# A product in the second bank of a PSUM pair, other banks for the last products, and two stores on GpSimd's queue

## Chip, cores and metric

The kernel runs on one core of a Trainium2 chip. The metric is the device time of one execution in microseconds (us), the median of several runs. A core has TensorE (PE in the profile, with PEld for its weight loads), VectorE (DVE), ScalarE (ACT), GpSimd (POOL) and SyncE (SP). Each works through its own list of instructions in order; an instruction waits for counts that the other engines and the DMA queues raise. SP, ScalarE and GpSimd issue DMAs on queues of their own.

## The reference

Retention over 8 batches of 576 positions and 8 heads of 64, then a feed-forward layer on the 4608 x 512 result:

```python
scores = scale * np.matmul(q, k.transpose(0, 1, 3, 2))
Dmat = np.where(rel >= 0, gamma[:, None, None] ** rel[None, :, :], 0.0)
x = np.matmul(scores * Dmat[None, :, :, :], v)      # then (B * S, H * D) = (4608, 512)
...
h = x @ w_in                                        # 4608 x 2048
s = np.sin(alpha * h)
g = h + s * s / (alpha + 1e-09)
return (g @ w_out).astype(np.float32)               # 4608 x 512
```

## The kernel before

The 4608 rows are taken in 9 blocks of 512 (block 8 holds the last 64 positions of all batches). Each block goes through 16 units, one for each 128 of the 2048 columns of h. A unit is: `project`, four matmuls of 128x512 into one PSUM bank (L562); `sine` on ScalarE (L570), which reads that bank; `square` on ScalarE or VectorE (L579, L581); and `product` on VectorE (L586), which reads the square and the bank again and writes g, transposed, to the tile gT.

The second matmul of the layer, g times w_out, is done for blocks 3 to 8 with seven products of half-size matrices instead of eight. The 512x512 result of a block is cut into four quarters, and product i is a group of 16 matmuls of 128x256 that takes a factor on the left made from gT and one on the right made from w_out (L671, `FACTORS` at L654). Left factors S1 to S4 are sums of quarters of gT, made on VectorE by `row_sum` (L652). `after_product` (L700) joins the products: after product 1, ScalarE copies it to the tile low (L703); after 6, VectorE writes mid = product 6 + low (L705); after 7, low is raised (L707); after 2, 3, 4 and 5, a result quarter goes to a store tile osb (ScalarE copy L718, or VectorE add L720) and from there to the output by two DMAs (L684 for the last block, else L688).

PSUM has eight banks. The tags op, h0, h1 and h2 are one bank each; m0 and m1 are pairs, tiles of two banks. The tag names a place: a new tile of a tag waits until the readers of the old one are done. Attention uses the pairs whole. `bank` (L549) gives a unit the first bank of a pair when its tag is m0 or m1; the second bank then lies idle.

Iteration n of the loop over blocks 3 to 8 does the units of block n and, from n = 4 on, the seven products of block n - 1 between them. In iterations 4 to 7 units 0 and 1 take m0 and m1 (`aside`, L1387), and the other units take h0, h1, h2 in turn. After the start of every second unit stands one product (`slots`, L1389): product 1 stands on TensorE behind the projection of unit 1, product 2 behind that of unit 3, product 6 behind that of unit 5. Product 1 takes op. Product 2 is summed onto it in the same bank, once ScalarE has copied product 1; the sum is then copied out by ScalarE. Product 6 takes op next, and 7 is summed onto it; then 5 with 3, and 4, use op in the same way.

Up to units 13 to 15 of an iteration the next block's attention runs too; its results leave PSUM by ScalarE copies (L120), so ScalarE comes late to the sines of the last units and of units 0 and 1 that follow.

Behind the loop (L1398 on) come the seven products of block 8, with the last row sums between them, in the order 2, 4, 1, 6, 7, 5, 3; product 3 is done and stored in two halves. The stores there go half on SP's and half on ScalarE's queue (`both`). In iteration 8, whose units end in the order 8, 9, 10, 11, unit 8 has m0, unit 9 h2, unit 10 h0 and unit 11 m1; the turn of the h banks goes on with h1, h2, h0.

The order of instructions on every engine is the order of the calls in the program; no scheduler changes it.

Of the kernel before, what the change touches and what calls it, by code (L numbers as in the profile page):

```python
# [10 lines left out]
F32 = mybir.dt.float32  # L11
# [25 lines left out]
def kernel(  # L37
# [18 lines left out]
    nc = tc.nc  # L56
# [4 lines left out]
    P = 128  # L61
# [24 lines left out]
    psum = ctx.enter_context(tc.tile_pool(name="p", bufs=1, space=bass.MemoryType.PSUM))  # L86
# [459 lines left out]
    ops = {}  # L546
    PART = {None: slice(0, 512), 0: slice(0, 256), 1: slice(256, 512)}

    def bank(tag):  # L549
        if tag[0] == "m":  # L550
            return psum.tile([P, 2, 512], F32, tag=tag, bufs=1, name="hps")[:, 0]
        return psum.tile([P, 512], F32, tag=tag, bufs=1, name="hps")

    def project(n, fc, tag, part=None):

        if n not in gT:
            gT[n] = work.tile([P, FC, 512], F16, tag="gT", bufs=2, name="gT")
        if (n, fc) not in hps_of:
            hps_of[n, fc] = [bank(tag), None]
        cols = PART[part]  # L560
        for a in range(KT):
            matmul(  # L562
                hps_of[n, fc][0][:, cols], w_in16[fc // 4][:, a, fc % 4 :: 4], xs[n][:, a, cols],
                start=(a == 0 and part != 1), stop=(a == KT - 1), skip_group_check=True,
            )
# [44 lines left out]
    def quarter(n, t, h, p):  # L610
        return gT[n][:, 8 * p + 4 * h : 8 * p + 4 * h + 4, 256 * t : 256 * t + 256]

    def w_quarter(h, e, p):
        return w_out16[:, 8 * p + 4 * h : 8 * p + 4 * h + 4, 256 * e : 256 * e + 256]
# [8 lines left out]
    def piece(name, p):  # L623
        tag = PIECES[name, p]
        if (name, p) not in pieces:
            if tag in ("raw3", "raw5", "xT1"):
                both = work.tile([P, 2, 4, 256], F16, tag=tag, bufs=1, name=name)
                for x in range(2):
                    pieces[name, x] = both[:, x]
            else:  # L630
                pieces[name, p] = work.tile([P, 4, 256], F16, tag=tag, bufs=1, name=f"{name}_{p}")
        return pieces[name, p]
# [11 lines left out]
    def row_sum(n, name, p, eng):  # L644
        a11, a12, a21, a22 = (quarter(n, t, h, p) for t in range(2) for h in range(2))
        out_, x, y, op = {
            "S1": lambda: (piece("S1", p), a11, piece("S2", p), ADD),
            "S2": lambda: (piece("S2", p), a22, a21, SUB),
            "S3": lambda: (a21, a11, a21, SUB),
            "S4": lambda: (piece("S4", p), a12, piece("S2", p), SUB),  # L650
        }[name]()
        return eng.tensor_tensor(out_, x, y, op)  # L652
# [6 lines left out]
    def part_product(n, i, tag, js=(0, 1), first=None):  # L659
        left, right = FACTORS[i]  # L660
        if tag is not None:
            parts[n, i] = bank(tag)
        else:
            parts[n, i] = parts[n, first]
        acc = parts[n, i]
        for j in js:
            for p in range(2):
                lhs = piece(left, p) if isinstance(left, str) else quarter(n, *left, p)
                rhs = piece(right, p) if isinstance(right, str) else w_quarter(*right, p)
                for x in range(4):  # L670
                    matmul(  # L671
                        acc[:, 256 * j : 256 * j + 256], lhs[:, x, 128 * j : 128 * j + 128], rhs[:, x],
                        start=(tag is not None and j == js[0] and p == 0 and x == 0),
                        stop=(p == 1 and x == 3), skip_group_check=True,
                    )

    def store(n, t, e, osb, js=(0, 1), issue=(nc.sync, nc.sync)):
        cols = slice(256 * e, 256 * e + 256)
        for r in range(2):
            if n == 8:  # L680
                b0 = 4 * t + 2 * js[0]
                dst = out.rearrange("(b s) d -> b s d", s=S)[b0 : b0 + 2 * len(js), 512:576, cols]
                dst = dst.rearrange("(j r) s d -> r s j d", r=2)
                issue[r].dma_start(dst[r], osb[halves(r), js[0] : js[-1] + 1])  # L684
            else:
                r0 = 576 * n + 256 * t + 128 * js[0]
                dst = out[r0 : r0 + 128 * len(js), cols].rearrange("(j i r) d -> r i j d", r=2, i=64)
                issue[r].dma_start(dst[r], osb[halves(r), js[0] : js[-1] + 1])  # L688
# [6 lines left out]
    def kept_tile(name):  # L695
        tag = {"low": "qT1", "mid": "u2"}[name]
        kept[name] = work.tile([P, 512], F32, tag=tag, bufs=1, name=name)
        return kept[name]

    def after_product(n, i, js=(0, 1), issue=(nc.sync, nc.sync), apart=False, more=False):  # L700
        acc = parts[n, i]
        if i == 1:
            nc.scalar.copy(kept_tile("low"), acc)  # L703
        elif i == 6:
            nc.vector.tensor_tensor(kept_tile("mid"), acc, kept["low"], ADD)  # L705
        elif i == 7:
            nc.vector.tensor_tensor(kept["low"], acc, kept["mid" if apart else "low"], ADD)  # L707
        else:
            t, e = {2: (0, 0), 3: (0, 1), 4: (1, 0), 5: (1, 1)}[i]
            cols = slice(256 * js[0], 256 * js[-1] + 256)  # L710
            if (n, i) not in kept:
                kept[n, i] = work.tile([P, 2, 256], F32, tag="osb", bufs=4, name="osb")
            osb = kept[n, i].rearrange("p j d -> p (j d)")
            source = kept["mid" if i == 3 else "low"]
            if more:
                nc.vector.tensor_tensor(kept["mid"], acc, kept["mid"], ADD)
            if i == 2 and not apart:
                nc.scalar.copy(osb[:, cols], acc[:, cols])  # L718
            else:
                nc.vector.tensor_tensor(osb[:, cols], acc[:, cols], source[:, cols], ADD)  # L720
            store(n, t, e, kept[n, i], js, issue)
# [60 lines left out]
    with tc.manual_schedule():  # L782
# [5 lines left out]
        first = work.tile([P, 1], F32, tag="first", bufs=1, name="first")  # L788
# [477 lines left out]
        h, m = cycle(("h0", "h1", "h2")), cycle(("m0", "m1"))  # L1266
        ON_A = (4, 5, 6, 8, 9, 10)
        for n in range(3, NBLK):
# [81 lines left out]
            def unit_start(i, u, tag):  # L1350
                project(n, u, tag)
                sine(n, u)
                for f in todo.get(i, []):
                    f()

            def unit_end(i, u, eng):
                if eng is not None:
                    square(n, u, eng)
                product(n, u)
                for f in after.get(i, []):  # L1360
                    f()
# [28 lines left out]
            for i in range(8):  # L1390
                for u in (2 * i, 2 * i + 1):
                    unit_start(u, units[u], aside.get(u) or next(h))
                    if u % 2 and slots[i] is not None:
                        k_ = slots[i]
                        part_product(n - 1, k_, None if k_ in (2, 7, 3) else "op", first={2: 1, 7: 6, 3: 5}.get(k_))
                        after_product(n - 1, k_)
                    unit_end(u, units[u], None if A and u == 13 else V if u in ON_V else A_)
        n = NBLK - 1  # L1398
        both = (nc.sync, nc.scalar)
        part_product(n, 2, "h0")  # L1400
        part_product(n, 4, "h1")
        row_sum(n, "S3", 1, V)
        row_sum(n, "S2", 1, V)
        part_product(n, 1, "op")
        after_product(n, 1)
        part_product(n, 6, "h2")
        row_sum(n, "S1", 1, V)
        after_product(n, 2, apart=True, issue=both)
        row_sum(n, "S4", 1, V)
        after_product(n, 6)  # L1410
        part_product(n, 7, "m0")
        after_product(n, 7, apart=True)
        part_product(n, 5, "h0")
        after_product(n, 4, issue=both)
        after_product(n, 5, more=True, issue=both)
        for j, tag in enumerate(("m1", "op")):
            part_product(n, 3, tag, (j,))
            after_product(n, 3, (j,), both)

# [29 lines left out]
```

## Time and profile before

| what | value |
|---|---|
| median of 3 runs | 300.42 us (300.3 to 303.47) |
| the profiled execution | 300.26 us |
| its span in the profile | 298.5 us |
| granted TensorE clock | 1.0 of full speed |
| DMA packets | 123431, 50.09 MB |

The span runs from the first to the last instruction of the program; the rest of the execution's time lies outside it. Times in the profile are microseconds from the span's start. A row of the timeline has start, length, engine, line, operation, tiles and shapes, how many instructions are merged in it, and in brackets how long the engine stood idle before it and what released it. Matmuls overlap: sixteen of 128x256 are shown with a length of 1.91 us but follow each other at a distance of 1.75 us for the group. SPq and ACTq rows are DMA issues; the length is that of the issue, not of the transfer. In the rows of waits stand the sum, the number and the longest.

### The profile page before, as it was taken

What the parts mean: (1) busy time and instruction counts of PE and PEld (TensorE: products, weight loads), DVE (VectorE), ACT (ScalarE), POOL (GpSimd) and SP (SyncE); (2) the same over time, 40 slices, a digit from 0 to 9 for tenths busy, and PEclk for the clock granted to TensorE, in tenths of its full rate; (3) what the DMA queues carried; (4) which work ended last, traced back from release to release, by engine and by line L of the source; (5) the groups of instructions that cost most, each with busy time, mean ns of one, the idle gap of its engine ahead of it and who ended that gap; (6) DMA issues with size and microseconds to landing.
All of it is one profiled execution on the core that took longest, in us unless ns stands there. A gap on an engine that the chain in (4) does not pass through costs nothing.

```text
span 298.5 us, 8497 instructions
## 1 busy us (share of the span) xinstructions
PE 285.1 (96%) x3480; PEld 184.0 (62%) x3480; DVE 226.6 (76%) x334; ACT 205.1 (69%) x343; POOL 136.3 (46%) x151
## 2 busy tenths in 40 slices
PE   6889999999998999999999999999999999999894
PEld 4666545555454645455777667767666776676583
DVE  2597878788259789687976787669778886977864
ACT  1579935997694877787768876877687657855500
POOL 5684688664788676550596059604940000000000
PEclk9999999999999999999999999999999999999999
DMA  7999999998796678998989887997763103111213
GB/s 210 347 234 209 252 292 316 254 265 234 174 249 164 146 165 178 264 168 178 131 207 183 180 172 186 174 153 178 170 137 91 40 12 78 35 37 35 70 37 107
DMA packets 123431, 50.09 MB, mean 168 GB/s; under 512 B 80384, under 2 KB 121344, under 8 KB 123392
## 3 DMA queue, kind: packets, MB, share of 16 engines
q1 hardware_dynamic: 119440, 44.78, 64.6%
q0 software_dynamic: 2688, 4.19, 7.7%
q10 hardware_dynamic: 1264, 0.58, 0.8%
q8 instruction: 27, 0.44, 0.6%
q14 instruction: 12, 0.10, 0.1%
HBM read 36.75 MB, written 9.44 MB: 155 GB/s over the span
## 4 chain that ended last, share of the span: by engine, by line
PE 77%; ACT 10%; DMA 5%; DVE 4%; issue 2%; SPq 0%; DVEq 0%; ACTq 0%
PE hps L562 35%; PE hps L671 23%; PE ops L605 10%; DMA raw<-in_v_dram 5%; ACT s L570 3%; PE o L427 2%; PE sc L385 2%; ACT xT L120 2%; ACT ss L579 2%; PE kv L321 2%; ACT v L120 1%; PE o L449 1%; DVE osb L720 1%; ACT kvs L120 1%; DVE ss L581 1%
## 5 line engine op out<-in xcount | busy, mean ns | idle before, releaser
L586 DVE SCALAR_TENSOR_TENSOR gT<-ss,inva,hps 128x512 f16<-128x512 f16 x144 | 105.7, 744 | 39.7 <-ACT ss L579 36.1
L570 ACT ACTIVATE s<-hps,alpha_t 128x512 f16<-128x512 f32 x144 | 97.0, 681 | 45.5 <-PE hps L562 45.1
L562 PE MATMUL hps<-xT,w_in 128*128 128x512 f16 (+1 forms) x532 | 121.1, 372 | 0.9 <-DVE ret L397 0.7
L562 PEld LDWEIGHTS <-w_in 128*128 128x128 f16 x596 | 66.6, 114 | 50.7 <-issue 1.4
L579 ACT ACTIVATE ss<-s 128x512 f16<-128x512 f16 x107 | 67.2, 630 | 2.8
L605 PE MATMUL ops<-w_out,gT 128*128 128x512 f16 x192 | 46.8, 380 | 0.0
L671 PEld LDWEIGHTS <-gT 128*128 128x128 f16 x384 | 37.5, 98 | 11.8 <-issue 3.9
L207 POOL TENSOR_TENSOR k<-raw,cn 128x1024 f16<-128x1024 f32 (+1 forms) x17 | 29.8, 1756 | 9.6 <-DMA raw<-in_k_dram 6.7
L671 PEld LDWEIGHTS <-S 128*128 128x128 f16 x288 | 27.7, 98 | 5.3
L605 PEld LDWEIGHTS <-gT 128*128 128x128 f16 x192 | 17.9, 98 | 20.4
L359 POOL TENSOR_TENSOR s<-kvs,cn 128x256 f16<-128x256 f32 x17 | 10.4, 614 | 40.4 <-DVE S L652 36.9
L207 POOL TENSOR_TENSOR q<-raw,cn 128x1024 f16<-128x1024 f32 x13 | 24.6, 1905 | 6.2 <-DMA raw<-in_q_dram 5.3
L671 PE MATMUL hps<-w_out,gT 128*128 128x256 f16 x192 | 22.9, 272 | 2.8 <-DVE gT L586 1.4
L671 PE MATMUL hps<-T,gT 128*128 128x256 f16 x192 | 22.9, 273 | 0.0
L671 PE MATMUL hps<-w_out,S 128*128 128x256 f16 x192 | 22.8, 273 | 0.0
L397 DVE TENSOR_TENSOR ret<-sc,mask 128x1024 f16<-128x1024 f32 x16 | 19.2, 1219 | 1.7 <-PE sc L385 1.7
L367 POOL TENSOR_TENSOR kvs<-s,kvs 128x256 f32<-128x256 f32 x21 | 16.7, 796 | 3.6 <-DVE kvs L122 1.1
L581 DVE TENSOR_TENSOR ss<-s 128x512 f16<-128x512 f16 x29 | 14.7, 509 | 3.1 <-ACT s L570 3.1
L366 POOL TENSOR_TENSOR s<-kvs,cn 128x256 f32<-128x256 f32 x21 | 13.1, 623 | 6.4 <-ACT kvs L120 6.2
L652 DVE TENSOR_TENSOR S<-gT,S 128x1024 f16<-128x1024 f16 x24 | 15.5, 684 | 0.0
L397 DVE TENSOR_TENSOR ret<-sc,mask_halved 128x768 f16<-128x768 f32 x16 | 15.2, 950 | 0.0
L562 PE MATMUL hps<-xS,w_in 128*128 128x512 f16 x64 | 15.1, 379 | 0.0
(82 smaller groups left out, 266.1 us busy)
## 6 DMA issues: line engine op xcount, KB each, us to landing
out_dram<-osb SPq DMA_DIRECT2D x67, 128.0 KB, 2.5
raw<-in_q_dram SPq DMA_DIRECT2D x16, 512.0 KB, 5.3
raw<-in_k_dram SPq DMA_DIRECT2D x8, 512.0 KB, 6.1
raw<-in_v_dram SPq DMA_DIRECT2D x8, 512.0 KB, 6.3
raw<-in_v_dram SPq DMA_DIRECT2D x32, 128.0 KB, 3.4
raw<-in_k_dram SPq DMA_DIRECT2D x32, 128.0 KB, 3.2
w_in<-in_moe_w_in_dram POOLq DMA_DIRECT2D x4, 512.0 KB, 11.7
w_out<-in_moe_w_out_dram POOLq DMA_DIRECT2D x4, 512.0 KB, 13.0
```

What stands on the lines that cost most here:

```text
L207: eng.tensor_tensor(dst[:, a0:a1].rearrange("p a r t d -> p t (a r) d"), t_.rearrange("p (t a) x -> p t a x", t=2)[:, :, a0:a1].rearrange( ...
L366: nc.gpsimd.tensor_tensor(s32, self.kvs[:, c - 1], g1.unsqueeze(2).to_broadcast([P, 4, D]), MULT)
L367: nc.gpsimd.tensor_tensor(self.kvs[:, c], s32, self.kvs[:, c], ADD)
L397: nc.vector.tensor_tensor(ret.rearrange("p t (z x) -> p (t z) x", z=2)[:, :, 0:n], sc.rearrange("p t (z x) -> p (t z) x", z=2)[:, :, 0:n], ...
L562: matmul(hps_of[n, fc][0][:, cols], w_in16[fc // 4][:, a, fc % 4 :: 4], xs[n][:, a, cols], start=(a == 0 and part != 1), stop=(a == KT - 1 ...
L570: nc.scalar.activation(s_t, hps, mybir.ActivationFunctionType.Sin, bias=0.0, scale=alpha_t[:, fc : fc + 1],)
L579: nc.scalar.activation(ss_t, s_t, mybir.ActivationFunctionType.Square)
L581: eng.tensor_tensor(ss_t, s_t, s_t, MULT)
L586: nc.vector.scalar_tensor_tensor(gT[n][:, fc, :], ss_t, inva[:, fc : fc + 1], hps, MULT, ADD)
L605: matmul(ops[n, c, cols.start][:, cols], gT[n][:, fk, c * P : (c + 1) * P], w_out16[:, fk, cols], start=(fk == 0), stop=(fk == FC - 1), sk ...
L652: return eng.tensor_tensor(out_, x, y, op)
L671: matmul(acc[:, 256 * j : 256 * j + 256], lhs[:, x, 128 * j : 128 * j + 128], rhs[:, x], start=(tag is not None and j == js[0] and p == 0 ...
```

## The change

Three edits:

- In iterations 4 to 7, product 1 of the block before goes to the second bank of the pair m1 whose first bank unit 1 holds. Product 2 is then a group of its own in op, and its quarter is made by a VectorE add of product 2 and low in place of the ScalarE copy.
- Behind the loop, products 2, 4, 6, 7, 5 and the first half of 3 take m0, three turns of the h banks, m1 and m0, in place of h0, h1, h2, m0, h0 and m1.
- Product 5's two stores behind the loop are both issued on GpSimd's queue.

```diff
+    pair = {}
+
     def bank(tag):
+        if tag == "m1 second":
+            return pair["m1"][:, 1]
         if tag[0] == "m":
-            return psum.tile([P, 2, 512], F32, tag=tag, bufs=1, name="hps")[:, 0]
+            pair[tag] = psum.tile([P, 2, 512], F32, tag=tag, bufs=1, name="hps")
+            return pair[tag][:, 0]
         return psum.tile([P, 512], F32, tag=tag, bufs=1, name="hps")
...
                     if u % 2 and slots[i] is not None:
                         k_ = slots[i]
-                        part_product(n - 1, k_, None if k_ in (2, 7, 3) else "op", first={2: 1, 7: 6, 3: 5}.get(k_))
-                        after_product(n - 1, k_)
+                        alone = n < 8 and k_ < 3
+                        tag = "m1 second" if alone and k_ == 1 else None if k_ in (2, 7, 3) and not alone else "op"
+                        part_product(n - 1, k_, tag, first={2: 1, 7: 6, 3: 5}.get(k_))
+                        after_product(n - 1, k_, apart=alone and k_ == 2)
...
         both = (nc.sync, nc.scalar)
-        part_product(n, 2, "h0")
-        part_product(n, 4, "h1")
+        part_product(n, 2, "m0")
+        part_product(n, 4, next(h))
...
-        part_product(n, 6, "h2")
+        part_product(n, 6, next(h))
...
-        part_product(n, 7, "m0")
+        part_product(n, 7, next(h))
         after_product(n, 7, apart=True)
-        part_product(n, 5, "h0")
+        part_product(n, 5, "m1")
         after_product(n, 4, issue=both)
-        after_product(n, 5, more=True, issue=both)
-        for j, tag in enumerate(("m1", "op")):
+        after_product(n, 5, more=True, issue=(nc.gpsimd, nc.gpsimd))
+        for j, tag in enumerate(("m0", "op")):
             part_product(n, 3, tag, (j,))
             after_product(n, 3, (j,), both)
```

Lines of the changed kernel stand 5 below those of the kernel before up to the loop: `sine` is L575 there, the product groups L676, low L708, the adds to osb L725, the last stores L689.

## The prediction

> **What bounds the kernel now.** I read the page first, then the stages, then TensorE's waits, then single stretches of the timeline. The page's header, the busy line, the chain, and two stages (start:end, length, PE, PEld, DVE, ACT, POOL busy, granted clock, DMA share, GB/s):
>
> ```profile
> span 298.5 us, 8497 instructions
> PE 285.1 (96%) x3480; PEld 184.0 (62%) x3480; DVE 226.6 (76%) x334; ACT 205.1 (69%) x343; POOL 136.3 (46%) x151
> PE 77%; ACT 10%; DMA 5%; DVE 4%; issue 2%; SPq 0%; DVEq 0%; ACTq 0%
> 137.00:268.00 131.00, 129.59 (x1576) 90.77 (x1575) 104.10 (x154) 98.82 (x161) 45.73 (x51) 1.00 0.64 131
> 268.00:298.50 30.50, 24.66 (x194) 19.11 (x191) 20.35 (x33) 8.80 (x14) 0.00 (x0) 1.00 0.23 61
> ```
>
> From 137 to 268 us, where most of the change lies, TensorE stands still for 131.00 - 129.59 = 1.41 us. So there any new TensorE wait is added to the time, and any wait removed comes off it, while a fraction of a microsecond on VectorE or ScalarE hides as long as TensorE need not wait for it. TensorE's waits from 150 us on are only these:
>
> ```profile
> PE hps L671 <- DVE gT L586: 1.4, 1, 1.4
> PE hps L671 <- DVE osb L720: 1.4, 3, 0.6
> ```
>
> Both are aimed at by the change: the three before product 1 (0.58, 0.57, 0.24) and the one at the end (1.43).
>
> **Part 1, product 1 in the second bank of unit 1's pair.** It happens in four iterations, n = 4 to 7. Before, product 1 writes "op" and waits there for VectorE's read of product 4. After, that wait goes. But the list of waits of the two built programs has, at product 1 of iteration 5, the same matmul with another wait:
>
> ```
> before: 4226 L671 Matmult hps<-w_out_74,gT 128x256 [waits DVE_49]
> after:  4226 L676 Matmult hps<-w_out_74,gT 128x256 [waits Activation_49]
> ```
>
> The ScalarE count asked for is the one that the sine of unit 1 reaches. The pair is one tile, and a write into its second half is ordered behind the read of its first half that stands before it in the program. The same holds in iterations 4, 6 and 7. So product 1 now starts when the sine of unit 1 ends. Timeline of TensorE's product 1, and of the sine that covers it, iteration by iteration (start, length, idle before and releaser):
>
> ```profile
> 138.31 1.91 PE L671 MATMUL hps<-w_out,gT 128*128 128x256 f16 x16
> 139.05 0.67 ACT L570 ACTIVATE s<-hps,alpha_t 128x512 f16<-128x512 f32 x1
> ...
> 167.58 0.68 DVE L720 TENSOR_TENSOR osb<-hps,low 128x512 f32<-128x512 f32 x1
> 168.32 1.91 PE L671 MATMUL hps<-w_out,gT 128*128 128x256 f16 x16 [0.58 <-DVE osb L720]
> 168.66 0.67 ACT L570 ACTIVATE s<-hps,alpha_t 128x512 f16<-128x512 f32 x1
> ...
> 198.32 1.91 PE L671 MATMUL hps<-w_out,gT 128*128 128x256 f16 x16 [0.57 <-DVE osb L720]
> 197.42 1.25 ACT L570 ACTIVATE s<-hps,alpha_t 128x512 f16<-128x512 f32 x2
> ...
> 227.34 1.91 PE L671 MATMUL hps<-w_out,gT 128*128 128x256 f16 x16 [0.24 <-DVE osb L720]
> 227.53 0.67 ACT L570 ACTIVATE s<-hps,alpha_t 128x512 f16<-128x512 f32 x1
> ```
>
> The sine of unit 1 ends at 139.72, 169.33, 198.67 and 228.20. The hand-over from the VectorE add (ends 168.26) to TensorE (168.32) took 0.06; I use 0.05 for one from ScalarE. New starts less old ones: 1.46, 1.06, 0.40 and 0.91, together 3.83 us later. The sine itself does not move: in ScalarE's order nothing ahead of it changes, and its own input, unit 1's projection, ends before the wait. The end of this projection is product 1's start less its wait (167.74, for example), so TensorE's new idle times are 1.46, 1.64, 0.97 and 1.15. Bounds: 3.4, if ScalarE, relieved of a copy below, comes to each of these places 0.1 earlier; 4.2, if the hand-over costs 0.1 more. I take 3.83.
>
> Behind the waiting matmul stand units 2 and 3 on TensorE; behind them ScalarE and VectorE, which have work of their own in that time. The product of unit 1 on VectorE (L586) gets a new wait too, for the end of product 1, since it reads the same pair. It costs nothing: it already follows the square of unit 1, which stands behind the copy of product 1 in ScalarE's order. The next user of m1, the scores of unit 5, waits for that copy, some 5 us old by then.
>
> **Part 2, product 2 on its own in "op".** Four ScalarE copies to the store tile become four VectorE adds. Rows of a grouping by line for 137 to 232 us, and of the tile low:
>
> ```profile
> L718 ACT COPY osb<-hps 128x512 f32<-128x512 f32 x3 | 1.8, 589 | 1.6 <-PE hps L671 1.6
> L720 DVE TENSOR_TENSOR osb<-hps,low x13: 681/691/694, 155.3 to 293.0; 128x512 f32<-128x512 f32 x13
> ```
>
> ScalarE loses 4 x 0.59, VectorE gains 4 x 0.69. What can wait for it is product 6, which takes "op" next. The tightest place is iteration 7, which has no scores between:
>
> ```profile
> 232.70 1.29 DVE L652 TENSOR_TENSOR S<-gT,S 128x1024 f16<-128x1024 f16 x2
> 234.28 0.93 PE L671 MATMUL hps<-T,S 128*128 128x256 f16 x7
> ```
>
> The new add follows these row sums, which end at 233.99; VectorE is put back by about 0.5 there (by the new wait of unit 1's product), so the add ends near 234.5 + 0.7 = 235.2. Product 6 would start at 234.28 + 0.91 = 235.19. A tie: 0, with 0.7 as the upper bound if all of the add showed. In iterations 4 to 6 the scores stand ahead of product 6, and it doesn't show.
>
> **Part 3, other banks for the last products.** The last block's product 2 took h0, which unit 10 still held. VectorE's products of units 8 and 10, TensorE's last units, the wait, the next row sum that a product needs, and the chain to the end:
>
> ```profile
> 277.36 0.75 DVE L586 SCALAR_TENSOR_TENSOR gT<-ss,inva,hps 128x512 f16<-128x512 f16 x1 [0.44 <-ACT ss L579]
> 280.91 0.74 DVE L586 SCALAR_TENSOR_TENSOR gT<-ss,inva,hps 128x512 f16<-128x512 f16 x1
> 278.38 1.89 PE L562 MATMUL hps<-xS,w_in 128*128 128x512 f16 x8
> 281.70 1.91 PE L671 MATMUL hps<-w_out,gT 128*128 128x256 f16 x16 [1.43 <-DVE gT L586]
> 284.75 0.69 DVE L652 TENSOR_TENSOR S<-gT 128x1024 f16<-128x1024 f16 x1
> 281.70 12.40 PE hps L671 x112
> 294.12 0.42 DVE osb L720
> ```
>
> Now product 2 takes m0, last held by unit 8, whose product ended at 278.11. So it starts when TensorE comes free, 281.70 - 1.43 = 280.27, and all 1.43 us go, if nothing is late next. Product 1 would start two groups (3.5 us) later, at 283.8; unit 11's product ended before. Product 6 would start at 285.5, and the second half of its S2 ends at 285.44, needed only after its first eight matmuls. The later banks (h0 to h2, m1, m0) were left long before. So VectorE's last add ends at 294.54 - 1.43 = 293.11.
>
> **Part 4, the fifth product's stores on GpSimd's queue.** Last adds, and the issues on the two queues before; the two GB/s rows cut 293.6:296.6 and 295.6:297.7 into 40 slices each:
>
> ```profile
> 292.99 0.68 DVE L720 TENSOR_TENSOR osb<-hps,low 128x512 f32<-128x512 f32 x1
> 293.70 0.60 SPq L684 DMA_DIRECT2D out_dram<-osb  x1
> 295.03 0.56 SPq L684 DMA_DIRECT2D out_dram<-osb  x1
> 294.43 0.81 ACTq L684 DMA_DIRECT2D out_dram<-osb  x1
> 295.33 0.55 ACTq L684 DMA_DIRECT2D out_dram<-osb  x1
> GB/s 191 164 191 218 219 315 355 396 410 232 82 14 0 0 0 0 0 0 137 218 232 205 205 218 137 205 260 355 396 396 355 369 383 287 164 191 205 191 314 246
> GB/s 313 351 410 390 371 351 390 391 332 351 196 156 156 176 254 234 195 312 293 312 390 332 313 215 215 59 59 0 0 0 0 0 0 0 0 0 156 0 0 0
> ```
>
> SP's store issued at 293.70 moves its first bytes at 294.95 (slice 19 of the first row): 1.25 us. The last bytes come at 297.0 (slice 27 of the second), the span ends 1.5 us behind them. Without product 5's stores in their queues, ScalarE's last issue comes at 293.1 + 0.35 (behind its 0.81) = 293.45 instead of 295.33: the hardware queues alone would end 1.88 earlier. The stores on GpSimd: the add ends at 293.67 - 1.43 = 292.24, the queue is idle. Its prices are seen only at the start of the kernel, last at 35 us; issue, then q0's and q1's packets in 36.3:37.5 and in 37.5:42.0:
>
> ```profile
> 35.23 0.60 POOL L113 DMA_DIRECT2D w_out<-in_moe_w_out_dram  x1
> q1 hardware_dynamic: 820, 0.42, 114.8%
> ...
> q0 software_dynamic: 144, 0.52, 58.6%
> DMA to landing us min/median/max: 7.0/13.0/15.8
> ```
>
> No q0 packet before 37.5, so 2.3 us from issue to first bytes, with every DMA engine full; at the end they are 23% busy. Bounds for the first bytes are thus 1.25 and 2.3; I take 2.0, nearer to the same queue. The second store is issued at 292.27 + 0.60 = 292.87, begins at 294.87, moves its 128 KB beside the others in about 1.0, ends at 295.9; with the 1.5 the span would end at 297.4, 1.15 before the present 298.54. So GpSimd's store is last, and Parts 3 and 4 together bring 1.15. Bounds: 1.88 (hardware queues last), and, with the 7.0 us of the shortest software transfer (four times the bytes, full engines), a loss of 2.3.
>
> The Trainium skill, DMA: Bandwidth & Descriptors, section on latency and other measured facts, puts the first byte about 0.4 us later from GpSimd's queue than from SP's (1 us against 0.6). By that the second store would end with the hardware ones and the end bring some 1.85, an estimate; the rows here have 1.25 and 2.3, and the sum goes by them.
>
> **Sum.** The profiled execution took 300.26 us, of which 298.54 is its span; the median shown is 300.42. 300.26 + 3.83 + 0 - 1.15 = 302.9.
>
> **Rivals.**
>
> A, the forecast, 0.60: own range 302.3 to 303.8; about 0.13 of it lies above 303.4.
>
> B, faster, 0.06: the second bank really is free of the sine, so product 1 starts at the end of unit 1's projection and the three waits go: 300.26 - 1.39 - 1.15 = 297.7, or 297.0 with the end of D. For it speaks that the halves are different banks. It decides wherever the matmul's wait is met before the projection ends; against it stands the wait in the list, and the sine ending 0.9 to 1.6 behind the projection in all four places. The Trainium skill, PSUM: Partial Sum Buffer, section on bank collisions, asks only for guarding by bank and quadrant, which this store would satisfy without any wait; no run here shows what the tile's bookkeeping adds.
>
> C, clearly slower, 0.22: GpSimd's second store lands late. From first bytes later than 2.5 us behind the issue, the total passes 303.4; a landing as late as the 7.0 us gives 300.26 + 3.83 + 2.3 = 306.4; half way 304.6. For it: the only software rows are slow ones. Against: full queues then, nearly empty ones at the end.
>
> D, 0.12: software stores as quick as SP's. The hardware queues end last, 300.26 + 3.83 - 1.88 = 302.2.
>
> **How the numbers follow.** A change of under 1% is about what a measurement of this kernel cannot tell from none; 1% of the median is 3.0 us, so the borders are 297.4 and 303.4. Slower: 0.22 + 0.13 = 0.35. B's 297.7 and 297.0 lie on both sides of the border: 0.04 of it is faster by over 1%, 0.02 within. Within: 0.47 of A, D's 0.12 and this 0.02, 0.61. The range 301.8 to 304.8 leaves out B, the far part of C (about 0.08) and a little of D: under 0.2.
>
> **What would show it.** Right: product 1 (part_product's line) waits for ACT s of 1.0 to 1.6 us in four places and never for DVE osb; no wait at the first product of the end; in the end GpSimd's DMA lands last. Wrong: product 1 without a wait (B); TensorE waiting for DVE osb at product 6 (Part 2 costs); the last bytes more than 3.5 us behind GpSimd's second issue (C), or ahead of ScalarE's (D).

## The result and the profile after

The changed kernel takes 304.48 us (median of 20 runs, 303.01 to 305.68); the kernel before, measured beside it, takes 300.97 (20 runs). The ratio is 1.0114, with a 95% interval from 1.0094 to 1.0133: slower by 1.1%, 3.5 us. Medians are of all executions; ratios leave out those that ran in a slower state.

The profiled execution of the changed kernel took 305.68 us. Its header, its busy line and its chain by engine:

```profile
span 304.0 us, 8502 instructions
PE 284.4 (94%) x3480; PEld 183.7 (60%) x3480; DVE 227.9 (75%) x338; ACT 203.2 (67%) x339; POOL 137.4 (45%) x153
PE 64%; DMA 14%; ACT 8%; POOL 4%; issue 3%; DVE 3%; SPq 3%; POOLq 0%; DVEq 0%; ACTq 0%
```

TensorE has the same 3480 matmuls and is busy no longer than before. DVE has four instructions more and ACT four fewer, which is Part 2. POOL has two more, product 5's stores.

Spans should not be compared whole here: the part ahead of iteration 4, which the change does not touch, ends anywhere from 136.6 to 141.9 us in the executions shown below. Stretches of half the TensorE clock ahead of it, which only some of them have, may be one reason (the mean clock of the first 20 us is 1.00 before the change and 0.83 after); this was not settled. So each trace is cut at three events: the first matmul of unit 0's projection in iteration 4, the last matmul of the last unit's projection in iteration 8, and the end of VectorE's last add. That gives three lengths: the stages, the products behind the loop, and the last stores. The windows of the kernel before, cut so, with start:end, length, busy time of PE, PEld, DVE, ACT and POOL, granted clock, DMA share and GB/s:

```profile
136.59:279.89 143.30, 141.88 (x1656) 99.17 (x1655) 113.06 (x170) 105.25 (x172) 45.73 (x51) 1.00 0.60 124
279.89:294.55 14.66, 12.77 (x114) 10.95 (x112) 11.53 (x19) 2.67 (x5) 0.00 (x0) 1.00 0.21 55
294.55:298.54 3.99, 0.00 (x0) 0.00 (x0) 0.00 (x0) 0.00 (x0) 0.00 (x0) 1.00 0.45 134
```

The same windows of the kernel after:

```profile
138.63:285.76 147.13, 141.96 (x1656) 99.04 (x1655) 115.49 (x174) 103.45 (x168) 45.73 (x51) 1.00 0.57 120
285.76:298.83 13.07, 12.61 (x114) 10.96 (x112) 11.53 (x19) 2.66 (x5) 0.59 (x1) 1.00 0.23 61
298.83:303.97 5.14, 0.00 (x0) 0.00 (x0) 0.00 (x0) 0.00 (x0) 0.70 (x2) 0.74 0.37 104
```

The stages grew by 3.83 us. Of this 3.75 is waiting; TensorE's shown busy time grew by only 0.08 (141.96 against 141.88). The products behind the loop lost 1.59. The last stores grew by 1.15. Together this is 165.34 against 161.95, 3.39 us longer; the medians differ by 3.51.

TensorE's waits from 137 us on in the kernel after, with sum, number and longest:

```profile
PE hps L676 <- ACT s L575: 5.1, 4, 1.7
```

There is one row only. The waits for DVE osb (1.4 in all) and for DVE gT at the end (1.4) are gone; four waits for the sine have come. Three of the four places in TensorE's timeline, with the sine that ends the second and the third of these waits:

```profile
141.81 1.91 PE L676 MATMUL hps<-w_out,gT 128*128 128x256 f16 x16 [1.29 <-ACT s L575]
172.15 0.67 ACT L575 ACTIVATE s<-hps,alpha_t 128x512 f16<-128x512 f32 x1
172.87 1.91 PE L676 MATMUL hps<-w_out,gT 128*128 128x256 f16 x16 [1.66 <-ACT s L575]
202.53 0.68 ACT L575 ACTIVATE s<-hps,alpha_t 128x512 f16<-128x512 f32 x1
203.26 1.91 PE L676 MATMUL hps<-w_out,gT 128*128 128x256 f16 x16 [1.03 <-ACT s L575]
```

Both sines end (172.82, 203.21) 0.05 us ahead of the matmul that they release.

### The profile page after: what moved, and what is told of

The parts are those of the page before. It is cut to its first block, busy times and chain, and to the rows that moved or that the text cites. A ratio compares the mean times of both kernels' runs of the same rounds, so it can differ in the third digit from the quotient of the medians.

```text
span 304.0 us, 8502 instructions
## 1 busy us (share of the span) xinstructions
PE 284.4 (94%) x3480; PEld 183.7 (60%) x3480; DVE 227.9 (75%) x338; ACT 203.2 (67%) x339; POOL 137.4 (45%) x153
## 4 chain that ended last, share of the span: by engine, by line
PE 64%; DMA 14%; ACT 8%; POOL 4%; issue 3%; DVE 3%; SPq 3%; POOLq 0%; DVEq 0%; ACTq 0%
PE hps L567 30%; PE hps L676 23%; PE ops L610 6%; DMA raw<-in_v_dram 5%; DMA raw<-in_k_dram 4%; ACT s L575 3%; DMA w_in<-in_moe_w_in_dram 3%; PE sc L385 2%; DMA qT<-q 2%; SPq L153 1%; ACT xT L120 1%; PE o L427 1%; POOL k L207 1%; ACT v L120 1%; SPq L158 1%
## 5 line engine op out<-in xcount | busy, mean ns | idle before, releaser
L575 ACT ACTIVATE s<-hps,alpha_t 128x512 f16<-128x512 f32 x144 | 96.9, 681 | 51.2 <-PE hps L567 50.8
L676 PEld LDWEIGHTS <-gT 128*128 128x128 f16 x384 | 37.5, 98 | 14.1 <-issue 6.3
L689 POOL DMA_DIRECT2D out_dram<-osb x2 | 1.3, 650 | 73.7 <-DVE osb L725 73.7
L676 PEld LDWEIGHTS <-S 128*128 128x128 f16 x288 | 27.7, 98 | 5.3
L676 PE MATMUL hps<-w_out,gT 128*128 128x256 f16 x192 | 22.9, 272 | 5.1 <-ACT s L575 5.1
L676 PE MATMUL hps<-T,gT 128*128 128x256 f16 x192 | 22.9, 273 | 0.0
L676 PE MATMUL hps<-w_out,S 128*128 128x256 f16 x192 | 22.8, 273 | 0.0
```

The source lines that it names most:

```text
L575: nc.scalar.activation(s_t, hps, mybir.ActivationFunctionType.Sin, bias=0.0, scale=alpha_t[:, fc : fc + 1],)
L676: matmul(acc[:, 256 * j : 256 * j + 256], lhs[:, x, 128 * j : 128 * j + 128], rhs[:, x], start=(tag is not None and j == js[0] and p == 0 ...
```

## The experiments

All lengths below are those of the three windows just described; "total" is their sum, 161.95 us before the change.

### The stages alone

Parts 1 and 2 as in the changed kernel, the end as before the change:

```diff
-        part_product(n, 2, "m0")
-        part_product(n, 4, next(h))
+        part_product(n, 2, "h0")
+        part_product(n, 4, "h1")
...
-        after_product(n, 5, more=True, issue=(nc.gpsimd, nc.gpsimd))
+        after_product(n, 5, more=True, issue=both)
```

> Parts 1 and 2 alone: product 1 in the second bank of unit 1's pair and product 2 on its own in iterations 4 to 7, the last block's products and stores as before. Theory (product 1 waits for the sine of unit 1, in all 5.1 us of TensorE waits in place of 1.4): +3.7 us, four waits of product 1 for ACT s of 1.0 to 1.7 us, none for DVE osb; the wait of 1.4 us at the first product of the end stays. Rival (part of the 3.4 us that the whole change cost comes from the end): +2.5 us or less.

Its first window and TensorE's waits:

```profile
141.03:288.17 147.14, 142.00 (x1656) 98.99 (x1655) 115.50 (x174) 103.46 (x168) 45.69 (x51) 1.00 0.59 121
```

```profile
PE hps L676 <- ACT s L575: 5.1, 4, 1.6
PE hps L676 <- DVE gT L591: 1.4, 1, 1.4
```

The stages take 147.14, 3.84 more than before; the other two windows are as before (14.66 and 3.98). Total 165.78. Timed: ratio 1.0142, 1.0088 to 1.0196. So the loss of the change sits in the stages, and the end of the changed kernel gives a little of it back.

### The end alone, and the end without GpSimd's stores

Two kernels with the stages of before: one has the whole new end (Parts 3 and 4), the other only the banks (Part 3), its last edit being

```diff
-        after_product(n, 5, more=True, issue=(nc.gpsimd, nc.gpsimd))
+        after_product(n, 5, more=True, issue=both)
```

> Parts 3 and 4 alone: other banks for the last products and product 5's stores on GpSimd's queue; iterations 4 to 7 as before. Theory (the removed wait gives 1.4 us, the stores on GpSimd's queue take 1.1 of it back): -0.3 us; VectorE's last add to the end of the span 5.1 us, against 4.0 before. Forecast of the prediction: -1.15 us.

> Part 3 alone: other banks for the last products, product 5's stores half on SP's and half on ScalarE's queue as before. Theory (the stores on GpSimd's queue cost the 1.1 us at the end): -1.4 us, VectorE's last add to the end of the span 4.0 us as before, no TensorE wait at the first product of the end. Rival (the end became longer because the products come earlier and the stores bunch): -0.3 us, the last add to the end 5.1 us.

The third window of the first, then the second and third of the other:

```profile
297.86:303.01 5.15, 0.00 (x0) 0.00 (x0) 0.01 (x1) 0.00 (x0) 0.71 (x2) 0.97 0.38 103
```

```profile
279.87:292.94 13.07, 12.61 (x114) 10.96 (x112) 11.52 (x19) 2.67 (x5) 0.00 (x0) 1.00 0.23 61
292.94:296.93 3.99, 0.00 (x0) 0.00 (x0) 0.00 (x0) 0.00 (x0) 0.00 (x0) 1.00 0.45 134
```

The banks bring 1.59 us between the loop and the last add and leave the stores at 3.99; GpSimd's queue adds 1.16 to the stores. Totals 161.54 and 160.35; timed, the ratios are 0.9969 (0.9941 to 0.9997) with both parts and 0.9900 (0.9859 to 0.9941) with the banks alone. Part 4 by itself is a loss.

### Product 1 in a tile of its own

Unit 1 takes an h bank, so that product 1 has m1 to itself; Part 2 stays, the end is that of the banks alone:

```diff
-            aside = {0: "m0", 1: "m1"} if n < 8 else {u: f"m{u // 3 % 2}" for u in range(0, 16, 3)}
+            aside = {0: "m0"} if n < 8 else {u: f"m{u // 3 % 2}" for u in range(0, 16, 3)}
...
-                        tag = "m1 second" if alone and k_ == 1 else None if k_ in (2, 7, 3) and not alone else "op"
+                        tag = "m1" if alone and k_ == 1 else None if k_ in (2, 7, 3) and not alone else "op"
```

> In iterations 4 to 7 unit 1 takes an h bank, and product 1 takes the pair m1 as a tile of its own, so that no reader of unit 1 stands in front of it; product 2 on its own in op as in the changed kernel; part 3 at the end, stores of product 5 on SP's and ScalarE's queues. Theory (the wait came from sharing the tile with unit 1): product 1 waits for nothing in iterations 4 to 7, -1.4 - 1.4 = -2.8 us. Rival 1 (the adds of product 2 on VectorE delay product 6 or the units behind): TensorE waits for DVE osb or DVE gT appear, and the gain is under 2 us. Rival 2 (the wait is one for ScalarE whatever the tile): product 1 still waits 1 us or more for ScalarE, and the time is above before.

Its first window, its waits, and the two places where TensorE waits:

```profile
139.44:282.18 142.74, 141.79 (x1656) 99.45 (x1655) 114.64 (x174) 103.44 (x168) 45.70 (x51) 1.00 0.58 124
```

```profile
PE hps L676 <- DVE osb L725: 0.9, 2, 0.6
```

```profile
207.78 1.91 PE L676 MATMUL hps<-T,S 128*128 128x256 f16 x16 [0.31 <-DVE osb L725]
236.57 1.91 PE L676 MATMUL hps<-T,S 128*128 128x256 f16 x16 [0.59 <-DVE osb L725]
```

Product 1 waits for nothing any more: with no other user of its tile, neither the sine nor the add of product 4 holds it. But the left factors in these rows are T and S, so this is product 6, waiting for VectorE's add of product 2, in iterations 6 and 7. The gain is 2.13 us and not the 2.8 of the theory: the waits of the first rival came. Total 159.82; timed 0.9957 (0.9923 to 0.9991).

### The same, with product 2 summed onto product 1

Products 1 and 2 share m1, and ScalarE copies their sum as before the change:

```diff
-                        alone = n < 8 and k_ < 3
-                        tag = "m1" if alone and k_ == 1 else None if k_ in (2, 7, 3) and not alone else "op"
+                        alone = n < 8 and k_ == 1
+                        tag = "m1" if alone else None if k_ in (2, 7, 3) else "op"
...
-                        after_product(n - 1, k_, apart=alone and k_ == 2)
+                        after_product(n - 1, k_)
```

> Unit 1's own product goes to a bank of the h ring, so that m1 is a tile by itself; products 1 and 2 are summed in it and ScalarE copies them out as before the change. The groups at the end stand in the changed kernel's banks, product 5 is stored from SP's and ScalarE's queues. The lengths are those from unit 0's projection of iteration 4 on, against 161.95 us before. Theory: with unit 1 in its own bank nothing holds product 1, and the waits of product 6 in the run with product 1 in a tile of its own (0.31 and 0.59 us, both for VectorE's add of product 2) came from the four added VectorE adds, which are gone here. No wait in front of a product from iteration 4 to 7; that stretch is 1.4 to 1.5 us shorter than before (the three waits of product 1 of 0.60, 0.61 and 0.23 us go), the end 1.6 us shorter, 3.0 us in all, ratio about 0.990. Rival: the adds are not the reason, VectorE is as late with what product 6 waits for: waits of 0.3 to 0.6 us at product 6 stay, 2.1 us in all, ratio about 0.993.

```profile
141.90:283.55 141.65, 141.61 (x1657) 99.18 (x1656) 112.79 (x170) 105.26 (x172) 45.80 (x51) 1.00 0.59 125
```

Now TensorE is busy in 141.61 of 141.65 us; no wait is left. The stages are 1.65 us shorter than before (the 1.42 of waits that they had and 0.27 less shown busy time, against 0.04 of idle time that is left) and 1.09 shorter than in the run above: the four VectorE adds of Part 2 were what product 6 waited for. Product 6 also has a bank here that product 2 did not use. But ScalarE's copy of the sum ends well before product 6 starts (208.20 and 209.88 us in iteration 6, 236.99 and 237.93 in iteration 7), so it would not have waited for that copy in the old bank either. Total 158.72, 3.23 less than before. Timed: 298.45 us median, ratio 0.9898 (0.9844 to 0.9951). By the windows it is the fastest version here; its timed ratio cannot be told from that of the banks alone (0.9900).

### Product 1 in the second bank of unit 0's pair

```diff
-        if tag == "m1 second":
-            return pair["m1"][:, 1]
+        if tag == "m0 second":
+            return pair["m0"][:, 1]
...
-                        tag = "m1 second" if alone and k_ == 1 else None if k_ in (2, 7, 3) and not alone else "op"
+                        tag = "m0 second" if alone and k_ == 1 else None if k_ in (2, 7, 3) and not alone else "op"
```

> Product 1 goes to the second bank of unit 0's pair in place of unit 1's; the groups at the end in the changed kernel's banks, product 5's stores on SP's and ScalarE's queues. Unit 0's pair is written ahead of unit 1's, and its last reader is VectorE's product for unit 0, whose end in the trace before stood at 141.15, 170.78, 201.24 and 230.26 us, where product 1 started at 138.31, 168.32, 198.32 and 227.34. Theory (a bank of a pair waits for all readers of the pair, whichever bank they read): product 1 waits for VectorE, 2.5 to 3.0 us in each of four iterations, some 11.3 us in all; with 1.6 us off at the end 9.7 us more than before, 171.7 us from unit 0's projection of iteration 4 on. Rival (only the bank that is read counts): the waits of before for VectorE's add remain, 0.60, 0.61 and 0.23 us, and it is 160.4 us. Second rival (the sine of unit 1 holds it anyway): waits as in the changed kernel, 5.1 us in all, 163.7 us.

TensorE's waits, their four places, and then the first window, the first microseconds behind three of the waits, and two microseconds out of the second of these stretches. The third figure from the end is the granted clock:

```profile
PE hps L676 <- DVE gT L591: 12.6, 4, 3.6
```

```profile
143.75 1.91 PE L676 MATMUL hps<-w_out,gT 128*128 128x256 f16 x16 [2.72 <-DVE gT L591]
176.26 2.30 PE L676 MATMUL hps<-w_out,gT 128*128 128x256 f16 x12 [3.10 <-DVE gT L591]
210.90 2.50 PE L676 MATMUL hps<-w_out,gT 128*128 128x256 f16 x11 [3.57 <-DVE gT L591]
244.53 2.31 PE L676 MATMUL hps<-w_out,gT 128*128 128x256 f16 x12 [3.22 <-DVE gT L591]
```

```profile
139.13:298.76 159.63, 146.99 (x1657) 101.10 (x1655) 115.73 (x174) 103.75 (x168) 45.70 (x51) 0.97 0.51 110
143.75:147.00 3.25, 3.25 (x23) 2.36 (x23) 0.71 (x2) 1.31 (x3) 0.00 (x0) 1.00 0.85 173
176.26:180.00 3.74, 3.74 (x18) 2.40 (x18) 0.55 (x1) 0.55 (x2) 0.00 (x0) 0.56 1.05 168
210.90:214.64 3.74, 3.74 (x18) 2.54 (x18) 0.55 (x1) 0.16 (x1) 0.00 (x0) 0.55 0.69 174
178.00:180.00 2.00, 2.00 (x9) 1.11 (x8) 0.00 (x0) 0.55 (x2) 0.00 (x0) 0.50 1.03 104
```

The releaser is the one that the theory named: VectorE's product for unit 0, which reads the other bank of the tile. So a write into one bank of a pair waits for those readers of the other that stand ahead of it in the program, and which unit holds the first bank decides what the wait costs. The size was missed. The four waits less the 1.4 of before make 11.2 us, as expected, but the stages are 16.33 longer. The other 5.1 are in TensorE's busy time (146.99 against 141.88): behind the waits of 3.10, 3.57 and 3.22 us the granted clock was 0.55 to 0.56 in the mean over 3.74 us (the window behind 3.22 is like the two shown). In each of these stretches it stood at 0.50 for 3.41 us (176.72 to 180.14, 210.86 to 214.27, 244.99 to 248.40), which loses 1.7 us each time. Behind the wait of 2.72 it stayed at 1.00; the last section says why that is not a matter of the wait's length alone. Total 176.72.

### Product 5 not stored, and one of its stores on GpSimd's queue

Both with the new banks and the stages of before. In the first, the quarter of the last block that product 5 makes is not written; in the second the two stores go to GpSimd and ScalarE:

```diff
-        after_product(n, 5, more=True, issue=both)
+        after_product(n, 5, more=True, issue=(nc.gpsimd, nc.scalar))
```

> The groups at the end in the changed kernel's banks, the stages as before the change; product 5's two stores of the last block are left out, so that one quarter of it is never written. From the last VectorE add to the end of the span it was 3.99 us with those stores on SP's and ScalarE's queues and 5.14 us with both on GpSimd's. Theory (a store of product 3 behind an empty queue lands earlier, and the changed kernel's stores on GpSimd's queue cost 1.9 us more than that saves): 3.2 to 3.4 us. Rival (product 3's own stores set the end by their latency alone, whatever stands ahead of them): 3.9 to 4.0 us, so that all of the 1.15 us is a cost of GpSimd's queue.

> The groups at the end in the changed kernel's banks, the stages as before the change; of product 5's two stores the first is issued by GpSimd and the second by ScalarE. Last add to end of span: 3.99 us with SP's and ScalarE's queues, 5.14 us with both on GpSimd's. Theory (the 4096-byte packets of GpSimd's stores, 159 to 400 ns each where a 1024-byte packet of the other stores takes 44 to 69 ns, hold the DMA engines against product 3's stores, so half of them costs half): 4.4 to 4.7 us. Rival (any use of GpSimd's queue there adds a fixed time, as its drain does): 5.0 to 5.2 us. Second rival (only GpSimd's second store, issued 0.66 us later, is late): 4.0 us.

The third window of each:

```profile
292.98:296.81 3.83, 0.00 (x0) 0.00 (x0) 0.00 (x0) 0.00 (x0) 0.00 (x0) 0.99 0.28 71
```

```profile
296.27:300.11 3.84, 0.00 (x0) 0.00 (x0) 0.00 (x1) 0.00 (x0) 0.08 (x1) 0.95 0.46 139
```

Leaving both stores out brings only 0.16 us, but not because they stood in nobody's way. In that run, what the DMAs moved from the last add to the end of the span, in 40 slices of 0.10 us, and two of SP's waits at the end (count, lengths in ns, starts of the first and the last):

```profile
GB/s 0 0 0 0 0 0 94 199 209 241 240 209 168 157 240 188 262 209 199 63 0 0 0 0 0 0 0 0 0 0 0 0 0 0 84 0 0 0 0 0
```

```profile
L1445 SPq EVENT_SEMAPHORE  x2: 28/28/28, 295.3 to 295.7; - x2
```

Product 3's last bytes come 2.0 us behind the last add (slice 19), where it is 2.5 with product 5's stores on the hardware queues. Of these 0.5 us only 0.16 reach the end: between the two waits SP stands still for some 0.4 us, here behind the last landing, and the experiment with one load more comes back to this stop. So product 3's stores did come earlier without product 5's ahead of them, as in the theory, and the rival, by which their own latency sets the end, does not hold, though its number came out.

With one store on GpSimd's queue the stores take 3.84, as long as with none of product 5 at all; the last bytes come 2.3 us behind the last add. Of the three expectations the second rival comes nearest, that only GpSimd's second store, issued behind its first, is late. That half of the stores costs half, and that any use of the queue costs a fixed time, are both out.

### GpSimd's two stores without product 3's

Product 3's four stores are left out of the end with GpSimd's queue:

```diff
-            after_product(n, 3, (j,), both)
+            after_product(n, 3, (j,), None)
```

(with None, nothing is stored).

> The end of the changed kernel with product 3's four stores left out, so that one quarter of the last block is never written; the stages as before the change. In the changed kernel GpSimd's first store landed 2.62 us after its issue and its second, issued 0.66 us later, 3.24 us after its own. Theory (the second is held by product 3's stores, as they are by it): alone it lands 2.4 to 2.65 us after its issue. Rival (GpSimd's queue is slow with a second store behind the first): 3.1 to 3.3 us after its issue, whatever else is stored.

GpSimd's two stores, in the changed kernel and then in this one:

```profile
L689 POOL DMA_DIRECT2D out_dram<-osb x2: 632/650/667, 298.2 to 298.9; - x2
DMA to landing us min/median/max: 2.6/2.9/3.2
```

```profile
L684 POOL DMA_DIRECT2D out_dram<-osb x2: 634/652/669, 295.7 to 296.4; - x2
DMA to landing us min/median/max: 2.4/2.5/2.6
```

In the changed kernel one store landed 2.6 us and the other 3.2 us behind its issue; alone, neither takes more than 2.6. So the second is not slow by itself. It is held by product 3's stores, and holds them, as SP's landings show. SP's stores from 292 us on in the run with the banks alone, then those of product 3 in the changed kernel:

```profile
L684 SPq DMA_DIRECT2D out_dram<-osb x3: 554/556/596, 292.1 to 293.4; - x3
...
DMA to landing us min/median/max: 2.3/2.3/2.4
```

```profile
L689 SPq DMA_DIRECT2D out_dram<-osb x2: 490/519/548, 298.3 to 298.9; - x2
...
DMA to landing us min/median/max: 2.7/3.1/3.4
```

Where product 5's store went on SP's queue too, the two stores with a landing on record took 2.3 and 2.4 us, and product 3's is the shorter; beside GpSimd's second store, product 3's took 2.7 and 3.4. What moved them together shows in the DMA rows from the last add to the end of the span, in 40 slices, first with the banks alone (slices of 0.10 us), then after (0.13 us):

```profile
GB/s 0 0 0 10 151 232 212 182 202 222 303 353 363 414 353 253 141 192 222 323 323 323 283 101 10 0 0 0 0 81 0 0 0 0 0 0 0 0 0 0
```

```profile
GB/s 0 0 0 0 0 349 166 143 349 135 32 143 278 397 294 151 412 151 396 191 206 159 87 24 0 0 0 0 0 0 0 0 0 0 0 0 63 0 0 0
```

The same 0.53 MB starts in slice 3 (some 0.3 to 0.4 us behind the last add) and ends in slice 24 (2.5 us) with the hardware queues; after the change it starts in slice 5 (0.65 us) and ends in slice 23 (3.1 us), slower on the way. GpSimd starts its first issue at 298.24 and, one queue having both, its second only at 298.90, behind the last add (298.83). SP's and ScalarE's last stores are issued at 298.89 and 298.91, so three stores set out together. On the hardware queues product 5's two stores were issued together, 0.86 us ahead of that add (SP at 292.08, the add's end at 292.94). Whether the meeting alone makes them slower or also GpSimd's larger packets (see the last section) was not separated.

### One load more on SP's queue

What remained was a stop on SP. Between two of its waits at the very end SP stands still for some 0.4 us, though nothing is left to wait for. Here are the two waits in question: before, and after (count, lengths in ns, starts of the first and the last):

```profile
L1444 SPq EVENT_SEMAPHORE  x2: 28/28/28, 296.5 to 296.9; - x2
```

```profile
L1451 SPq EVENT_SEMAPHORE  x2: 28/28/28, 302.5 to 302.9; - x2
```

Before, this lies 0.7 us ahead of the end of SP's wait for the last landing (297.58) and costs nothing. After, it lies behind the last landing, and all that ends the program comes later by it. In every trace the stop stands in front of SP's 336th instruction, counted from its first; one store less on SP's queue, with the wait ahead of it (343 instructions for 345), puts it two waits further towards the end. This kernel is the end alone with one idle load added in the last stage:

```diff
                     unit_end(u, units[u], None if A and u == 13 else V if u in ON_V else A_)
+                    if n == 8 and u == 13:
+                        fill_up()
```

> The end of the changed kernel (banks, product 5's stores on GpSimd's queue), the stages as before the change, and one small load more on SP's queue in the last stage, long before the end, which nothing reads. In every trace so far SP stands still for 0.40 us ahead of its 336th instruction, where its other waits at the end follow each other by 0.06 to 0.08 us. With 345 instructions on SP that place lies between two landings of stores and costs nothing; with 343, as in the changed kernel, it lies behind the last landing. Theory (the place is fixed by the count of SP's instructions): with one or two instructions more it moves ahead of the last landing, and from the last VectorE add to the end of the span it is 4.75 to 4.85 us, against 5.15 us with the same stores. Rival (the stop belongs to the last landing or to GpSimd's queue): 5.1 to 5.2 us.

```profile
295.71:300.55 4.84, 0.00 (x0) 0.00 (x0) 0.00 (x0) 0.00 (x0) 0.71 (x2) 0.79 0.40 110
```

4.84, where the same stores took 5.15 and 5.14. The stop is again in front of the 336th instruction, now while a store is still under way. A load that does nothing makes this end 0.3 us faster; total 161.22, against 161.54 without it.

## Why the prediction was right

302.9 us was forecast and 304.48 measured: slower, as forecast, and inside the range, but by 1.1%, where the likeliest case stood just within 1%. Of the 1.54 us between the two, 0.71 is the starting point: the sum begins at 300.26, and the kernel before, measured beside the change, took 300.97. Another 0.71 is the end, where Parts 3 and 4 brought 0.44 instead of 1.15. The steps came out unevenly.

- **Part 1** was forecast at +3.83 and measured at +3.83 to +3.84, and not by luck: counted from the start of the stages, the four places put product 1 off by 1.46, 1.05, 0.39 and 0.92 us, and 1.46, 1.06, 0.40 and 0.91 were forecast. The idle times, 1.46, 1.64, 0.97 and 1.15 in the forecast, are shown as 1.29, 1.66, 1.03 and 1.15. The mechanism is shown twice: take the other user out of the tile and the wait goes; put product 1 beside unit 0 instead of unit 1 and it waits for unit 0's last reader. Rival B, that the second bank is free of the sine, is out. By the Trainium skill, PSUM: Partial Sum Buffer, section on bank collisions, guarding per bank and quadrant would do; the waits here go by the tile, and cost 5.1 us.
- **Part 2** was called a tie, at 0 with a bound of 0.7. In the changed kernel it is that tie: in iteration 7 VectorE's add of product 2 ends at 240.10 and product 6 starts at 240.15 without a shown wait. It holds only because product 1's wait puts TensorE off. Without that wait Part 2 costs 0.9 us (0.31 and 0.59), and 1.09 in the length of the stages. Naming product 6 in iteration 7 as the tightest place was right; that it does not show in iterations 4 to 6 held in the changed kernel, but not for iteration 6 in the run with the tile of its own.
- **Part 3** was forecast at -1.43 and measured at -1.59. Nothing was late next. A shown wait counts from the modelled end of the last matmul, and the ends are drawn late, since the matmuls overlap: TensorE's busy time in that window also fell, from 12.77 to 12.61, which is the other 0.16.
- **Part 4** is the term that was mis-sized: Parts 3 and 4 together were put at -1.15, so Part 4 at +0.28, and it cost +1.15 to +1.16. From the last add to the end of the span 4.29 us was forecast (293.11 to 297.4), and 5.14 came. The larger part of the miss is the stretch from the last bytes to the end, which was carried over at 1.5 us and became 2.0; 0.3 of that is SP's stop. The other part is the last bytes, 3.14 us behind the last add in place of 2.79. GpSimd's second store itself began almost when forecast, 1.69 us behind the last add for 1.76, but by luck, since two errors cancel. Its issue was put 0.3 too early (the first issue starts 0.29 behind the adds that it waits for and lasts 0.67), and its first bytes were taken 2.0 us behind the issue and came 1.62 behind it (the first store's 1.25, the lower bound). What the sum put at nothing is the price for the others: the store's bytes were to move "beside the others in about 1.0", and ScalarE's and SP's last bytes came at 3.14 and 3.13, behind GpSimd's at 2.96. By the prediction's own list GpSimd's bytes ahead of ScalarE's were a sign of rival D.
- **Rivals C and D** both miss as mechanisms, though half of C's way (304.6) is next to the measured time: its first bytes later than 2.5 us did not come, nor a landing later than 3.24. For D the first bytes were quick enough, as the Trainium skill, DMA: Bandwidth & Descriptors, section on latency and other measured facts, suggests with about 1 us for GpSimd's queue (here 1.25 and 1.62). By that the end was to gain 1.85; it gained 0.44, because the price was not in the first bytes. (With the page's 0.4 us on top of SP's 1.25 the prediction's own working gives some 1.5, an estimate, and not 1.85.) D's own end, 1.88 us earlier with the hardware queues alone, comes out as 1.75 in the run without product 5's stores (1.59 and 0.16).

Of the 1.15 us of Part 4, 0.64 is the later last bytes (3.14 against 2.50), 0.3 SP's stop, and some 0.2 stays open: two more of SP's waits stand behind the last landing than before, at 0.06 to 0.08 each, but that was not tried by itself. Nor was it tried what SP does in its stop.

## What to carry to other kernels

A free bank inside a tile that something else uses is not free: a write into it is ordered behind every reader of the tile that stands ahead of it in the program. So give it a tile of its own (no wait here), or put it beside the neighbour whose reads ahead of it are over first (5.1 us beside unit 1, 12.6 beside unit 0). A wait that is removed has to be followed to the next user of the same engine: the four adds of Part 2 cost nothing as long as product 1 waited, and 0.9 us once it did not. At the end of this kernel the last landing counted, and what SP still had to do behind it. Two stores behind each other on GpSimd's queue brought the second into the way of those that were already last; one store there cost nothing.

## What was not expected of the hardware

- TensorE's granted clock fell to 0.50 for 3.41 us at a time, and the length of a wait did not decide it. The falls in the run with unit 0's pair, at 176.72, 210.86 and 244.99 us, are ten times 3.41 us apart, as if the clock were set anew every 3.41 us. In the 3.41 us ahead of each TensorE was idle for 2.95, 3.41 and 2.96. The wait of 2.72 fell across such a border (at 142.59), with 1.56 on one side and 1.16 on the other, and the clock stayed at 1.00. The other runs agree: a wait of 2.04 us that lay within one such window (GpSimd's stores without product 3's, up to 91.11 us) was followed by 3.41 us at 0.50, and one of 2.75 us that lay across a border (the stages alone, 1.92 of it in the window up to 93.45) was not. So far the least idle time in a window that brought the slow clock is 2.04 us, and the most that did not is 1.93. The Trainium skill, TensorE: Matmul & The Clock Gate, part on the clock gate, has half the clock after an idle window of some 3.4 us and full clock after a busy one of the same length; the length agrees, but not all of the windows here were idle throughout. Each fall in the run with unit 0's pair cost 1.7 us beyond the wait.
- SP stood still for about 0.4 us in front of its 336th instruction in all twelve traces, whatever stood there. One store less on SP's queue shifted that place behind the last landing.
- GpSimd's two stores were written in packets of 4096 bytes of 159 to 409 ns each (the run with the load more), where the hardware queues' packets beside them had 1024 bytes and 44 to 142 ns.
